# Where an attention and MLP kernel's buffers begin: first transfers on one queue, ten products of zeros, weights in one buffer each, and starts at multiples of 512 bytes

## The chip, the cores and the metric

The kernel runs on one core of one Trainium2 chip. The metric is the device time of one launch in microseconds (us), the median of several runs. A measurement of this kernel can tell about 0.3% from no change.

## What is computed

Everything is float32. With x of 2048 rows and 448 columns, 16 heads of 28 columns:

```python
g = sigmoid((x * gate_w).sum(-1, keepdims=True))
qkv = (x @ wqkv)                      # 448 -> 3 * 448, split into q, k, v of 16 heads
p = softmax(q @ k.T * 28 ** -0.5)     # per head, 2048 x 2048
a = concat_heads(p @ v) @ wo
y = layernorm(x)
b = gelu(y @ w1 + b1) @ w2 + b2       # 448 -> 1792 -> 448
out = g * a + (1 - g) * b
```

## The kernel before, in words

**Split numbers.** Most products run in the `F32R` type. An operand is kept as two parts, a rounded high part (`...h`) and the rest (`...l`), and a product is the sum of three: high by high, high by low, low by high. The 448 rows of a weight are laid out as 4 tiles of 128 rows; the last tile holds 64 rows twice, so that its low part lies in its own upper half and a sum of products takes 11 matrix products (three for each of tiles 0 to 2, two for tile 3), not 12. ScalarE makes the high parts, VectorE or GpSimd the low parts.

**Stages, in the order in which TensorE runs them** (TensorE's order, and in most stages that of all engines, is the order of the program text):

1. `WARM` = 8 products of zeros (L275 to L276), 128 by 128 float32, while the first transfers run.
2. q and k of the first 512 rows (L301 to L335). Seven tiles `m` of 128 weight columns (`wh[m]`, `wl[m]`) are multiplied by the four tiles `t` of x transposed (`xh[0]`, `xl[0]`). The order follows the arrival of the pieces: w0, x0, w1, x1, w2, x2, w3, x3, w4, w5, w6. `fetch_wqk` (L176) and `fetch_x` (L193) issue the transfers, all on SyncE's queue (SP) except x0, which goes on ScalarE's queue (L289). `split_wqk` (L180) and `split_x` (L197) make the parts.
3. The rest of q and k (`qk_tile`, L215, products at L222, 512 columns) and v (`v_tile`, L225, products at L234, 450 columns: 448 of v and one of the gate). q, k, v go to DRAM. VectorE takes the statistics of the layer norm meanwhile.
4. The MLP in four chunks of 512 rows: `mlp1` (L604, products at L612, 512 columns) and `mlp2` (L619, products at L625, L626, L630, 448 columns). Between them a "filler" (`RowMax`, L381) already computes the row maxima of the attention scores: products of 28 rows at L440, which VectorE reduces (L420, L422).
5. Attention in 16 blocks (4 groups of heads, 4 chunks of queries): scores in three products (L563, 28 or 29 rows; four heads lie in four groups of 32 rows and run beside each other), exponentials on ScalarE (L567), the rest of the filler, and probabilities by v (L828, plain float32).
6. The output projection (`project`, L725, products at L733 to L735, 448 columns) and the gate.

**Where the buffers lie.** Each `tile(...)` is a buffer with the same range of bytes in all 128 partitions. A pool stacks its buffers in the order in which the program makes them, each rounded up to 32 bytes, from the left end of the memory or (`side="right"`) from the right end. Before, this gives, in bytes of a partition:

- left: four small constants from 16384, `const` from 16512 to 18336, then `qx`, `qo`, `qw` and, later in the same place, the pools of the MLP and of attention. 18336 is 416 past a multiple of 512. So `raw`, `xh`, `xl`, `hl` (and later `hh`, `hl`, `h`, `pt`, `w2h`) start 416 past one, `wvh` too, `wvl` 448 past one, and the rows `t` of `wvh` and `wvl` follow each other at 1800 bytes. `wh0`, `wl0`, `wh1`, ... come after three small buffers (`st`, `mv`, `mr`) and start 96 past a multiple of 512. `w2l` and the results of attention (`oh0` to `ol2`) start 160 past one, since they follow buffers with rows of 1792 bytes.
- right: `khr` at 215392 (352 past a multiple of 512), and so `qd`, the `w1f` buffers, the two `y`, and in attention `khi`, `klo`, `qh`, `ql`, `vg`, all 352 past one.

Every start before is thus a multiple of 32 but, apart from `wvl`, of no larger power of two.

**What the MLP's buffers lie on.** The pools of the MLP reuse the bytes of `qx`, `qo`, `qw`; a buffer's first write waits until the last use of what lay there. `hh0`, the first one that `mlp1` writes (L615), lies over the last bytes of `qw`.

The lines that set the order of the first transfers and the zeros:

```python
zeros = spare(NF - 1)[:, 0, :P]
nc.vector.memset(zeros, 0.0)
for _ in range(WARM):
    nc.tensor.matmul(bank[:, 0, :P], zeros, zeros, start=True, stop=True)
...
for what, i in turns:
    if what == "w":
        fetch_wqk(i)
    else:
        fetch_x(0, i, nc.sync if i else nc.scalar)
```

Of the kernel before, what the change touches and what calls it, by code (L numbers as in the profile page):

```python
# [7 lines left out]
F32 = mybir.dt.float32  # L8
F32R = mybir.dt.float32r
AF = mybir.ActivationFunctionType  # L10
# [5 lines left out]
P = 128  # L16
# [6 lines left out]
CH = 512  # L23
# [4 lines left out]
NM = 2 * D // P  # L28
# [3 lines left out]
MLP_G = MLP_MAX // 260  # L32
MG = 6
FS = 4
WARM = 8
W1, W2 = 0.233, 0.205
LQ = 12
STEPS = (2, 5, 7, 8, 9, 10)
# [4 lines left out]
def kernel(ctx: ExitStack, tc: tile.TileContext, xt, wqk, wv, wo, xk, w1, b1, w2, b2,  # L43
                          ident_d, sel_d, out):
    nc = tc.nc

    const = ctx.enter_context(tc.tile_pool(name="const", bufs=1))
# [6 lines left out]
    gate = const.tile([P, NT], F32, name="gate")  # L54
    ngate = const.tile([P, NT], F32, name="ngate")
    zall = const.tile([P, NT], F32, name="zall")
    nc.vector.memset(eps_t, EPS)


# [9 lines left out]
    nc.vector.memset(one_t, 1.0)  # L69


    mpool = ctx.enter_context(tc.tile_pool(name="mpool", bufs=2, side="right"))

    khr = mpool.tile([P, S], F32R, name="khr", bufs=1)
# [83 lines left out]
    with tc.tile_pool(name="qx", bufs=2) as qx, tc.tile_pool(name="qo", bufs=4) as qo, \  # L158
# [3 lines left out]
        def next_ps():  # L162
            nonlocal nps
            nps += 1
            return bank[:, nps % 8]

        def raw():
            return qx.tile([P, CH], F32, name="raw", bufs=6)
# [2 lines left out]

            return mw1.tile([P, 2, CH], F32, name=f"w1f{i}")

        wh, wl, wt = {}, {}, {}

        def fetch_wqk(m):  # L176
            wt[m] = halves.pop(0).rearrange("p (t x) -> p t x", t=4)
            nc.sync.dma_start(wt[m], wqk[m])

        def split_wqk(m):  # L180
            wh[m] = qw.tile([P, 4, P], F32R, name=f"wh{m}")
            wl[m] = qw.tile([P, 4, P], F32R, name=f"wl{m}")
            nc.scalar.activation(wh[m], wt[m], AF.Copy)
            nc.gpsimd.tensor_sub(wl[m], wt[m], wh[m].bitcast(F32))

        wvh = qw.tile([P, 4, 450], F32R, name="wvh")
        wvl = qw.tile([P, 4, 450], F32R, name="wvl")
        vt = [qw.tile([P, H, 32], F32, name=f"vt{i}") for i in range(3)]

        xh, xl = {}, {}  # L190
        xraw = {}

        def fetch_x(c, t, queue=nc.sync):  # L193
            xraw[c, t] = raw()
            queue.dma_start(xraw[c, t], xt[t, :, c * CH:(c + 1) * CH])

        def split_x(c, t):  # L197
            if t == 0:
                xh[c] = qx.tile([P, 4, CH], F32R, name="xh")
                xl[c] = qx.tile([P, 3, CH], F32R, name="xl")  # L200
            r = xraw.pop((c, t))
            nc.scalar.activation(xh[c][:, t], r, AF.Copy)
            if t < 3:
                nc.vector.tensor_sub(xl[c][:, t], r, xh[c][:, t].bitcast(F32))
            else:
                nc.vector.tensor_sub(xh[c][64:128, t], r[64:128], xh[c][64:128, t].bitcast(F32))

        def qk_out(c, m, ps):
            hl = qo.tile([P, 2, CH], F32R, name="hl")
            nc.scalar.activation(hl[:, 0], ps, AF.Copy)  # L210
            nc.vector.tensor_sub(hl[:, 1], ps, hl[:, 0].bitcast(F32))
            nc.sync.dma_start(qk[:, m * P:(m + 1) * P, c * CH:(c + 1) * CH].rearrange("n p t -> p n t"),
                              hl.bitcast(F32))

        def qk_tile(c, m):  # L215
            ps = next_ps()
            ops = []
            for t in range(3):
                ops += [(wh[m][:, t], xh[c][:, t]), (wh[m][:, t], xl[c][:, t]), (wl[m][:, t], xh[c][:, t])]
            ops += [(wh[m][:, 3], xh[c][:, 3]), (wl[m][:, 3], xh[c][:, 3])]  # L220
            for i, (a, b) in enumerate(ops):
                nc.tensor.matmul(ps, a, b, start=(i == 0), stop=(i == len(ops) - 1))  # L222
            qk_out(c, m, ps)
# [50 lines left out]
# [3 lines that stand above are left out]
# [8 lines left out]
        for what, i in turns:  # L285
            if what == "w":
                fetch_wqk(i)
            else:
                fetch_x(0, i, nc.sync if i else nc.scalar)  # L289
        wvr = []  # L290
        for t in range(4):
            wvr.append(halves.pop(0)[:, :450])
# [1 line left out]
        for t in range(2):  # L294
            fetch_x(1, t)
# [3 lines left out]
        banks = [next_ps() for m in range(NM)]  # L299
        there, pieces, late, count = [], [], [], [0] * NM  # L300
        for what, i in turns:  # L301
            if what == "w":
                if i < 4:
                    split_wqk(i)
                there.append(i)
                new = [(i, t) for t in pieces]
            else:
                split_x(0, i)
                pieces.append(i)
                new = [(m, i) for m in there]  # L310
            ops = [("hh", m, t) for m, t in new]

            low, late = late + [("lh", m, t) for m, t in new], []
            if what == "w":
                late = [x for x in low if x[1] == i]
            ops += [x for x in low if x not in late]
            ops += [("hl", m, t) for m, t in new if t < 3]
            if i == NM - 1:
                ops += late
            for k, m, t in ops:  # L320
                a, b = wl[m] if k == "lh" else wh[m], xl[0] if k == "hl" else xh[0]
                nc.tensor.matmul(banks[m], a[:, t], b[:, t], start=(count[m] == 0), stop=(count[m] == 10))  # L322
                count[m] += 1
                if m == 0 and count[m] == 11:

                    for n in range(4, NM):
                        split_wqk(n)
                    for n in range(4):
                        nc.scalar.activation(wvh[:, n], wvr[n], AF.Copy)
                        nc.gpsimd.tensor_sub(wvl[:, n], wvr[n], wvh[:, n].bitcast(F32))  # L330
                if count[m] == 11:
                    qk_out(0, m, banks[m])
                    if m in (1, 3):
                        split_x(1, m // 2)
                        fetch_x(1, m // 2 + 2)  # L335
# [34 lines left out]
        for n in range(NM, 11 * NC):  # L370
            for what, a in ahead[n]:
                what(*a)
            c, m = divmod(n, 11)
            if m < NM:
                qk_tile(c, m)
            else:
                v_tile(c * TPC + m - NM)
            for what, a in behind[n]:
                what(*a)
# [218 lines left out]
    hh, hl = {}, {}  # L598
# [234 lines left out]
    with tc.manual_schedule(engines=ENGINES):  # L833
# [7 lines left out]
        while u < 4 * steps:  # L841
# [4 lines left out]
            while at < units[-1] // 4:  # L846
                at += 1
                n, k = divmod(at, NT)
                g, c = divmod(n, NC)
# [111 lines left out]
```

## Time and profile before

| | |
|---|---|
| median of 3 runs | 1117.81 us (1117.55 to 1120.91) |
| the profiled execution | 1117.1 us, its span 1115.3 us |
| granted TensorE clock | 1.0 |
| VectorE (DVE), busy share of the span | 66% |
| ScalarE (ACT), busy share | 57% |
| GpSimd (POOL), busy share | 30% |
| DMA, mean rate over the span | 76 GB/s |

The span is the time from the first to the last instruction; the 1.8 us beside it lie outside the program. A row of the chain of waits reads: start, time, engine, output buffer, line, count; `PE bank L222 x76` are 76 products of line 222 that followed each other with nothing between. Time divided by count is the **pace**: the distance from one product to the next. The profile's own duration of one product is longer than its pace, because a product starts while the one before still drains. A row of the timeline reads: start, time, engine, line, operation, output and inputs, count, and in brackets the idle time before it with what ended it. `SPq` and `ACTq` are transfers that an engine's queue issues. A float32 product at `F32` appears as two rows.

### The profile page before, as it was taken

How to read it: one execution, taken by the hardware profiler on the slowest of the kernel's cores; microseconds unless marked ns; L12 is line 12 of the kernel's file. 1: busy time of each engine (PE TensorE's matmuls, PEld its weight loads, DVE VectorE, ACT ScalarE, POOL GpSimd, SP SyncE). 2: the span in 40 equal slices, each digit the busy share in tenths (PEclk: the TensorE clock that was granted, in tenths of full speed). 3: DMA queues.
4: the chain of work that ended last, by engine and by line, in shares of the span. 5: the costliest groups of instructions: out<-in, count | busy, mean ns of one | idle time of the engine just before them, and what ended most of it. 6: DMA issues, size and time to landing. Idle time of an engine off the chain costs nothing.

```text
span 1115.3 us, 19794 instructions
## 1 busy us (share of the span) xinstructions
PE 1106.8 (99%) x8152; PEld 674.9 (61%) x8152; DVE 741.2 (66%) x1030; ACT 634.8 (57%) x660; POOL 334.0 (30%) x354
## 2 busy tenths in 40 slices
PE   9999999999999999999999999999999999999998
PEld 7888777777777777744444444444444444454546
DVE  4553398988888889576766766666667767746103
ACT  5334651330231232287887887887878878847572
POOL 5016664242344231013112221320223024342350
PEclk9999999999999999999999999999999999999999
DMA  7988641011121023162100220012021003002011
GB/s 247 363 266 284 179 122 53 9 47 36 50 55 37 25 53 87 41 166 79 28 19 20 61 72 19 21 28 52 26 59 37 18 20 94 12 26 69 34 53 58
DMA packets 53079, 84.35 MB, mean 76 GB/s; under 512 B 8516, under 2 KB 28500, under 8 KB 52076
## 3 DMA queue, kind: packets, MB, share of 16 engines
q1 hardware_dynamic: 48588, 76.01, 22.2%
q0 software_dynamic: 4256, 6.81, 2.3%
q8 instruction: 64, 1.05, 0.4%
q10 hardware_dynamic: 144, 0.26, 0.1%
q14 instruction: 27, 0.22, 0.1%
HBM read 56.40 MB, written 26.49 MB: 74 GB/s over the span
## 4 chain that ended last, share of the span: by engine, by line
PE 98%; DVE 1%; ACT 1%; DMA 0%; issue 0%; ACTq 0%
PE bank L828 22%; PE bank L563 20%; PE bank L440 16%; PE bank L612 13%; PE bank L222 5%; PE bank L630 5%; PE bank L625 4%; PE bank L626 4%; PE bank L234 3%; PE bank L322 2%; PE bank L733 1%; PE bank L734 1%; PE bank L735 1%; DMA w1f<-in_wqk 0%; ACT khi L567 0%
## 5 line engine op out<-in xcount | busy, mean ns | idle before, releaser
L567 ACT ACTIVATE pt<-bank 128x1536 f32<-128x1536 f32 (+1 forms) x386 | 460.3, 1243 | 121.7 <-PE bank L563 121.7
L420 DVE TENSOR_REDUCE mx<-bank 128x1 f32<-128x512 f32 x618 | 409.8, 688 | 174.0 <-PE bank L440 160.1
L828 PE MATMUL bank<-pt,vg 128*32 128x512 f32 x1942 | 260.4, 602 | 0.0
L422 DVE TENSOR_REDUCE mx<-bank 128x2 f32<-128x1024 f32 x203 | 238.9, 1220 | 30.3 <-PE bank L440 30.0
L440 PE MATMUL bank<-khi,qd 28*128 28x512 f32 x512 | 241.9, 480 | 0.1
L440 PEld LDWEIGHTS bank<-khi,qd 28*128 28x128 f32 x512 | 92.3, 181 | 148.1 <-DVE mx L420 104.4
L563 PE MATMUL bank<-qh,klo 28*128 28x512 f32 x1024 | 174.2, 394 | 0.0
L563 PE MATMUL bank<-qh,khi 29*128 29x512 f32 x768 | 156.3, 480 | 0.8 <-ACT khi L567 0.6
L612 PE MATMUL bank<-y,w1f 128*128 128x512 f32 x616 | 151.9, 397 | 0.0
L612 PEld LDWEIGHTS bank<-y,w1f 128*128 128x128 f32 x616 | 112.6, 188 | 33.1 <-issue 10.8
L563 PE MATMUL bank<-ql,khi 28*128 28x512 f32 x768 | 128.8, 390 | 0.0
L617 POOL TENSOR_TENSOR hl<-h,hh 128x512 fp32r<-128x512 f32 x56 | 72.5, 1295 | 117.6 <-ACT h L616 77.4
L615 ACT ACTIVATE hh<-bank,b1s 128x512 fp32r<-128x512 f32 x56 | 38.7, 691 | 98.6 <-PE bank L612 98.6
L828 PEld LDWEIGHTS bank<-pt,vg 128*32 128x32 f32 x1942 | 44.6, 108 | 78.7 <-issue 78.3
L563 PEld LDWEIGHTS bank<-qh,klo 28*128 28x128 f32 x1024 | 87.2, 185 | 3.6
L636 ACT ACTIVATE h<-bank 128x448 f32<-128x448 f32 x16 | 8.7, 546 | 137.9 <-PE bank L630 103.6
L749 POOL DMA_DIRECT2D lt<-ob x15 | 10.9, 727 | 253.0 <-DVE ob L748 253.0
L630 PE MATMUL bank<-w2h,hl 128*128 128x448 f32 x224 | 85.0, 379 | 0.0
L563 PEld LDWEIGHTS bank<-qh,khi 29*128 29x128 f32 x768 | 60.6, 181 | 39.8 <-ACT pt L567 25.0
L625 PE MATMUL bank<-w2h,hh 128*128 128x448 f32 x224 | 83.3, 372 | 0.0
L626 PE MATMUL bank<-w2l,hh 128*128 128x448 f32 x224 | 81.9, 366 | 0.0
L440 PE MATMUL bank<-khr,qd 28*128 28x512 f32 x512 | 80.3, 467 | 0.5 <-issue 0.3
(135 smaller groups left out, 1298.0 us busy)
## 6 DMA issues: line engine op xcount, KB each, us to landing
qk<-hl SPq DMA_DIRECT2D x28, 512.0 KB
vs<-vt SPq DMA_DIRECT2D x16, 256.0 KB
s<-in_xt SPq DMA_DIRECT2D x16, 256.0 KB
raw<-in_xt SPq DMA_DIRECT2D x15, 256.0 KB
rc<-rls POOLq DMA_DIRECT2D x60, 64.0 KB, 2.2
w1f<-in_xk SPq DMA_DIRECT2D x8, 448.0 KB
gbs<-h SPq DMA_DIRECT2D x16, 224.0 KB
klo<-qk SPq DMA_DIRECT2D x16, 224.0 KB
```

The costliest lines, as they stand in the source:

```text
L222: nc.tensor.matmul(ps, a, b, start=(i == 0), stop=(i == len(ops) - 1))
L420: nc.vector.reduce_max(self.mx[:, c0:c0 + 1], bank[:, b0], axis=AX)
L422: nc.vector.reduce_max(self.mx[:, c0:c1 + 1:c1 - c0], bank[:, b0:b1 + 1], axis=AX)
L440: nc.tensor.matmul(bank[:, b], self.qds[self.n][r, i * P:(i + 1) * P], khi[self.n // NC][r, k * 512:(k + 1) * 512], start=True, stop=True)
L563: nc.tensor.matmul(bank[:, p], a[r, k * P:(k + 1) * P], b[r], start=(i == 0), stop=(i == 2))
L567: nc.scalar.activation(t, bank[:, at[0]:at[-1] + 1], AF.Exp, scale=SCALE)
L612: nc.tensor.matmul(ps, a, b, start=(i == 0), stop=(i == len(ops) - 1))
L617: nc.gpsimd.tensor_sub(hl[f], h, hh[f].bitcast(F32))
L625: nc.tensor.matmul(a, hh[f][:, sl], w2h[f], start=(f == 0), stop=False)
L626: nc.tensor.matmul(a, hh[f][:, sl], w2l[f], start=False, stop=False)
L630: nc.tensor.matmul(a, hl[f][:, sl], w2h[f], start=False, stop=(f == NF - 1))
L828: nc.tensor.matmul(pv[32 * j:32 * j + 32, :], vg[n // NC][:, k, 32 * j:32 * j + 32], probs.pop(4 * step + j), start=(k == 0), stop=(k == N ...
```

## The change

- `WARM` goes from 8 to 10.
- `fetch_x` loses its `queue` argument: x0 is issued on SP's queue too, between w0 and w1.
- `wh` and `wl` become one buffer each, `[P, NM, 4, P]`, made before `wvh`; product and split take the slice `[:, m]` or `[:, m, t]`.
- `wvh` and `wvl` are made with rows of 512 elements (2048 bytes), of which 450 are used.
- An unused buffer of 96 bytes ends `const`, and an unused pool of 352 bytes begins the right side. `qx` then starts at 18432 and `khr` at 215040, both multiples of 2048. All the buffers listed above with 416, 352, 96 or 448 start at a multiple of 512; `w2l` and `oh0` to `ol2`, behind rows of 1792 bytes, start 256 past one. The small buffers `st`, `mv`, `mr` and the rows of the layer norm now end `qw`, with `vt0` to `vt2` before them, so `hh0` lies over `vt2`.

The number, the order and the operands of all other instructions stay as they are.

```diff
-WARM = 8
+WARM = 10
...
     zall = const.tile([P, NT], F32, name="zall")
+    const.tile([P, 24], F32, name="pad")
...
+    ctx.enter_context(tc.tile_pool(name="edge", bufs=1, side="right")).tile([P, 88], F32, name="edge")
     mpool = ctx.enter_context(tc.tile_pool(name="mpool", bufs=2, side="right"))
...
-        wh, wl, wt = {}, {}, {}
+        wh = qw.tile([P, NM, 4, P], F32R, name="wh")
+        wl = qw.tile([P, NM, 4, P], F32R, name="wl")
+        wt = {}
...
         def split_wqk(m):
-            wh[m] = qw.tile([P, 4, P], F32R, name=f"wh{m}")
-            wl[m] = qw.tile([P, 4, P], F32R, name=f"wl{m}")
-            nc.scalar.activation(wh[m], wt[m], AF.Copy)
-            nc.gpsimd.tensor_sub(wl[m], wt[m], wh[m].bitcast(F32))
-
-        wvh = qw.tile([P, 4, 450], F32R, name="wvh")
-        wvl = qw.tile([P, 4, 450], F32R, name="wvl")
+            nc.scalar.activation(wh[:, m], wt[m], AF.Copy)
+            nc.gpsimd.tensor_sub(wl[:, m], wt[m], wh[:, m].bitcast(F32))
+
+        wvh, wvl = (qw.tile([P, 4, CH], F32R, name=f"wv{x}")[:, :, :450] for x in "hl")
...
-        def fetch_x(c, t, queue=nc.sync):
+        def fetch_x(c, t):
             xraw[c, t] = raw()
-            queue.dma_start(xraw[c, t], xt[t, :, c * CH:(c + 1) * CH])
+            nc.sync.dma_start(xraw[c, t], xt[t, :, c * CH:(c + 1) * CH])
...
-                ops += [(wh[m][:, t], xh[c][:, t]), (wh[m][:, t], xl[c][:, t]), (wl[m][:, t], xh[c][:, t])]
-            ops += [(wh[m][:, 3], xh[c][:, 3]), (wl[m][:, 3], xh[c][:, 3])]
+                ops += [(wh[:, m, t], xh[c][:, t]), (wh[:, m, t], xl[c][:, t]), (wl[:, m, t], xh[c][:, t])]
+            ops += [(wh[:, m, 3], xh[c][:, 3]), (wl[:, m, 3], xh[c][:, 3])]
...
-                fetch_x(0, i, nc.sync if i else nc.scalar)
+                fetch_x(0, i)
...
-                a, b = wl[m] if k == "lh" else wh[m], xl[0] if k == "hl" else xh[0]
-                nc.tensor.matmul(banks[m], a[:, t], b[:, t], start=(count[m] == 0), stop=(count[m] == 10))
+                w, x = wl if k == "lh" else wh, xl[0] if k == "hl" else xh[0]
+                nc.tensor.matmul(banks[m], w[:, m, t], x[:, t], start=(count[m] == 0), stop=(count[m] == 10))
```

## Prediction

> **What bounds the kernel now.** First the page: the busy times, then the chain that ended last.
>
> ```profile
> PE 1106.8 (99%) x8152; PEld 674.9 (61%) x8152; DVE 741.2 (66%) x1030; ACT 634.8 (57%) x660; POOL 334.0 (30%) x354
> ...
> PE 98%; DVE 1%; ACT 1%; DMA 0%; issue 0%; ACTq 0%
> PE bank L828 22%; PE bank L563 20%; PE bank L440 16%; PE bank L612 13%; PE bank L222 5%; PE bank L630 5%; PE bank L625 4%; PE bank L626 4%; PE bank L234 3%; PE bank L322 2%; PE bank L733 1%; PE bank L734 1%; PE bank L735 1%; DMA w1f<-in_wqk 0%; ACT khi L567 0%
> ```
>
> TensorE is the chain, from its first real product to the end. So time can come from two places only: the few us before it runs without a gap, and the pace of its products. The pace is read from the chain of waits in windows in which one stage runs alone (start, us, what, count):
>
> ```profile
> 10.90 14.20 PE bank L322 x62
> ```
> ```profile
> 26.24 7.80 PE bank L234 x38
> ```
> ```profile
> 35.28 17.74 PE bank L222 x76
> ```
> ```profile
> 65.98 13.05 PE bank L222 x57
> ```
> ```profile
> 116.35 14.76 PE bank L612 x65
> ```
>
> Time by count: L322 229.0 ns, L234 (450 columns) 205.3, L222 233.4 and 229.0, L612 227.1 ns. The projection (448 columns) from the first and the last of 37 steps of the timeline:
>
> ```profile
> 1103.46 0.37 PE L734 MATMUL bank<-wol,oh 128*128 128x448 f32 x1
> ...
> 1110.97 0.37 PE L735 MATMUL bank<-woh,ol 128*128 128x448 f32 x1
> ```
>
> 7.51 / 37 = 203.0 ns. Is that the array's own speed? The start of the program tells:
>
> ```profile
> 8.76 0.63 PE L322 MATMUL bank<-xl,wh 128*128 128x512 f32 x1
> ...
> 9.19 1.01 PE L322 MATMUL bank<-xh,wh 128*128 128x512 f32 x2
> ...
> 10.04 0.86 PE L322 MATMUL bank<-xh,wl 128*128 128x512 f32 x3
> ```
>
> Up to 10.04 us a product of 512 columns takes 0.43 us, behind it about 0.229 with the same buffers: the clock steps up. Half of 0.427 is 213.5 ns. If the step doubles the clock, which I take from these two paces, the array needs 213.5 ns, and 13.6 (L612) to 19.9 ns (L222) of each pace is an excess that the slow clock hides. Something that doesn't speed up with the array, such as the reading of operands, may set it. 213.5 ns for the 2048 bytes of a row is 6.67 ns for 64 bytes; in this unit the excess is 2.0 for L612, 2.3 to 3.0 for L222, 2.4 for L733 to L735 (186.8 ns by columns) and 2.7 for L234 (187.6).
>
> **The change, part by part.**
>
> *Starts at multiples of 512 (or 256).* A row of 2048 bytes that begins 32 past a multiple of 64, as all of them do before, covers 33 pieces of 64 bytes instead of 32, one of 1792 bytes 29 instead of 28. If reading goes by such pieces, a product loses one unit, 6.67 ns. v's rows of 1800 bytes cover 29 pieces from each old and new start: nothing there. No row of before has a 512-column product on an aligned operand, so the price is unknown; the bounds are nothing and the whole excess, 13.6 ns and more, and below nothing as in the last rival. I take one unit, as it is what the layout itself gives. How many products:
>
> ```profile
> L222 PE MATMUL bank<-xh,wh 128*128 128x512 f32 x84 | 33.4, 397 | 0.0
> L222 PE MATMUL bank<-xh,wl 128*128 128x512 f32 x84 | 33.2, 395 | 0.0
> L222 PE MATMUL bank<-xl,wh 128*128 128x512 f32 x63 | 24.9, 395 | 0.0
> ```
> ```profile
> L612 PE MATMUL bank<-y,w1f 128*128 128x512 f32 x616 | 151.9, 397 | 0.0
> L630 PE MATMUL bank<-w2h,hl 128*128 128x448 f32 x224 | 85.0, 379 | 0.0
> ...
> L440 PE MATMUL bank<-khr,qd 28*128 28x512 f32 x476 | 63.2, 466 | 0.5 <-issue 0.3 <-DVE mx L422 0.2
> ```
>
> L222 has 231, L322 77 (7 x 11 in the text), L612 616, L625, L626 and L630 three times 224, L733 to L735 three times 64: 1788 products of 128 rows, one behind the other. 1788 x 6.67 ns = 11.9 us.
>
> The products of 28 rows are less sure. One group of attention:
>
> ```profile
> 587.71 0.72 PE L563 MATMUL bank<-qh,khi 29*128 29x512 f32 x4
> 588.05 0.62 PE L563 MATMUL bank<-qh,klo 28*128 28x512 f32 x4
> ...
> 588.99 0.49 PE L440 MATMUL bank<-khi,qd 28*128 28x512 f32 x1
> 589.40 1.06 PE L828 MATMUL bank<-pt,vg 128*32 128x512 f32 x8
> 590.40 0.50 PE L440 MATMUL bank<-khi,qd 28*128 28x512 f32 x1
> ```
>
> Several heads run at once, and the 2.69 us of the group hold steps of 0.34 and 0.41 us at the changes of shape, which no start explains. With one unit in each of 7 levels of the about 205 groups (3072 products of L563 by 15) it would be 9.6 us, in the MLP's 476 filler products 3.2 us. Between 0 and 12.8 us I take 0, because beside the 128-row products nothing shows here what a level waits for; 12.8 stays in the range.
>
> What hides a gain: VectorE in the MLP, ScalarE in attention.
>
> ```profile
> 201.00:379.00 178.00, 178.00 (x911) 133.35 (x909) 157.71 (x165) 43.69 (x71) 66.63 (x52) 1.00 0.14 39
> 480.00:985.00 505.00, 504.93 (x4782) 237.77 (x4775) 346.95 (x550) 403.95 (x342) 124.29 (x171) 1.00 0.17 44
> ```
>
> The busy times are those of TensorE, its loads, VectorE, ScalarE, GpSimd. VectorE has 157.71 of 178 us in the MLP, so TensorE can gain 11% there before the filler's reductions are late; ScalarE 403.95 of 505 in attention. One unit is 3%.
>
> *First transfers and zeros.*
>
> ```profile
> 0.72 0.40 ACTq L195 DMA_DIRECT2D raw<-in_xt  x1
> ...
> 0.72 0.86 SPq L178 DMA_DIRECT2D w1f<-in_wqk  x2
> ...
> 1.20 3.78 PE L276 MATMUL bank<-w1f 128*128 128x128 f32 x16 [1.20 <-DVE w1f L274]
> ...
> 5.15 0.63 ACT L183 ACTIVATE wh<-w1f 128x512 fp32r<-128x512 f32 x1 [2.71 <-DMA w1f<-in_wqk]
> ...
> 5.69 0.61 ACT L202 ACTIVATE xh<-raw 128x512 fp32r<-128x512 f32 x1
> ...
> 6.36 0.79 PE L322 MATMUL bank<-xh,wh 128*128 128x512 f32 x1 [1.37 <-ACT xh L202]
> 6.83 0.63 ACT L202 ACTIVATE xh<-raw 128x512 fp32r<-128x512 f32 x1
> ```
>
> x0 is now issued 0.43 us later, and the SP transfers behind it by as much; w0 no longer shares its first us. ScalarE waits for w0 until 5.15 us, x0 is there when its turn comes. The first product can come up to 0.35 us earlier, or 0.1 us later if x0 is late. Two more zeros are four rows of at most 3.78 / 16 = 0.24 us: they end by 5.9 us, ahead of 6.36, so they delay nothing; the idle 1.4 us shrink. If the clock's step then comes earlier, the 6.6 products between 7.2 and 10.04 us save 0.2 us each, 1.3 us at most. Sum between -1.6 and +0.1; I take -0.5 us.
>
> *One buffer for wh, for wl.* No instruction is added. A wait could be: a split of `wh[:, 1]` behind the products of `wh[:, 0]`. But `xh` is such a buffer already, and at 6.83 ScalarE writes its second slice without idle time, half a us after the first product began to read the first. Nothing.
>
> *hh0 over vt2.*
>
> ```profile
> 114.12 0.55 ACT L236 ACTIVATE vt<-bank 128x448 f32<-128x448 f32 x1 [1.19 <-PE bank L234]
> 116.44 0.55 ACT L236 ACTIVATE vt<-bank 128x448 f32<-128x448 f32 x1 [1.77 <-PE bank L234]
> ...
> 118.91 0.69 ACT L615 ACTIVATE hh<-bank,b1s 128x512 fp32r<-128x512 f32 x1 [0.63 <-PE bank L612]
> ```
>
> vt2 holds v tile 14, written until 114.67; its transfer has 4.2 us until `hh0` is written. Were it late, ScalarE's later work queues behind L615, but only the third tile of L612, 2.5 us later, needs that bank again. Nothing.
>
> The sum against the profiled execution's 1117.1 us (span 1115.3 and 1.8 beside it, 0.7 below the median): 1117.1 - 11.9 - 0.5 = 1104.7; with the 0.7, **1105.4 us**.
>
> **The rivals.**
>
> *Starts don't matter (0.28).* v's own rows speak for it: they start 0, 8, 16 and 24 bytes past a multiple of 32 for its four tiles.
>
> ```profile
> 28.34 0.37 PE L234 MATMUL bank<-wvh,xh 128*128 128x450 f32 x1
> ...
> 28.95 0.37 PE L234 MATMUL bank<-wvh,xh 128*128 128x450 f32 x1
> ...
> 29.57 0.36 PE L234 MATMUL bank<-wvh,xh 128*128 128x450 f32 x1
> ...
> 30.18 0.37 PE L234 MATMUL bank<-wvh,xh 128*128 128x450 f32 x1
> ```
>
> Three products take 0.61, 0.62, 0.61 us: no tile is faster. And L222 has 233.4 and 229.0 ns with the same weights' buffers, so part of the excess moves with unmoved starts. Against it: all old starts are alike modulo 64, and 1800 bytes can't show the piece. Then only the start is left: 1117.8 - 0.5 = 1117.3 us. The Trainium skill, "SBUF — State Buffer", Specifications (TRN2), gives lines of 16 bytes, of which each new one costs something. By that rule starts at multiples of 32 lose nothing, and the change gives this rival's time; the equal tiles of v agree.
>
> *The whole excess goes (0.12).* Then about two units leave every product: 1788 + 176 + 476 + 205 x 7 = 3875 x 13.3 ns = 51.5 us, 1065.8 us with the start. For it: 2.0 units of L612 are all alike. Against: v's 2.7 units, and the two paces of L222. The Trainium skill, "TensorE: Matmul & The Clock Gate", Back-to-back issue gap, gives 512 / 2.4 + 2.5 = 216 ns for a 512-column product (an estimate from its formula); the trace's 227.1 to 233.4 differ, and by the page the rest is removable.
>
> *Both operands begin at the same place and get in each other's way (0.20).* With all starts at 0 of 512, the weights' load and the moving operand of each product read the same place at once. Price: the slow pace of L222, 3.0 units, everywhere: L612 616 x 6.3 ns = 3.9, the 448-column ones 864 x 3.8 = 3.3, L222 about 0.4, and one unit in fillers and levels 12.8: 20.4 us, 1138 us; without the last, 1125. It decides if L612 goes from 227 to above 230. Against it: `y` and `w1f` both start at 352 of 512 already, and theirs is the fastest pace; `xh` (416) and `wh` (96) differ, and theirs is the slowest.
>
> **How the numbers follow.** The forecast, one unit in the 128-row products and up to that in the others (1090 to 1114), has 0.40. A measurement can tell about 0.3%, 3.4 us, from no change. Faster is 0.40 + 0.12, same 0.28, slower 0.20. The range of 8 in 10 runs from 1062, which cuts off the low end of the second rival, to 1127, which holds the mild form of the last and leaves out its full form.
>
> **What would show it.** Right: L612 at about 220 ns and L222 at 223 to 227, L733 to L735 at 196, L234 unchanged at 205; the first product by 6.4 us. L612 still at 227 and L222 at 229 to 233 are the first rival, 214 to 216 the second, L612 over 230 the third. In attention a group's 2.69 us tells whether the levels gain. Wrong I would be above all if the excess belongs to the change of weights between products, whose loads (x8152) stand beside every product.

## The result, and the profile after

The changed kernel takes 1115.51 us (median of 17 runs, 1115.0 to 1120.98); the kernel before takes 1117.81 us beside it (17 runs, 1116.15 to 1120.91). The ratio is 0.998, with a 95% interval of 0.9970 to 0.9989. So it is faster by 2.3 us, not by the 12.4 us of the forecast. The interval doesn't reach 1, but 2.3 us are less than the 0.3% (3.4 us) that the prediction took as the least that a measurement can tell. The profiled execution took 1115.45 us, its span is 1113.7 us; that is 1.6 us less than the profiled execution of before, while the medians lie 2.3 us apart. The lines named here have moved by one: L222 is now L223, L612 is L613.

The page of the changed kernel, busy times and chain:

```profile
PE 1105.7 (99%) x8156; PEld 675.7 (61%) x8156; DVE 745.5 (67%) x1030; ACT 634.8 (57%) x660; POOL 333.3 (30%) x354
...
PE 96%; DVE 2%; DMA 1%; ACT 1%; issue 0%; POOL 0%; SPq 0%; ACTq 0%; DVEq 0%
```

TensorE is still the chain; 4% of it belong to others, where it was 2%. Its paces, from the chain of waits in windows of one stage (start, us, what, count):

```profile
25.01 8.95 PE bank L235 x44
```
```profile
33.96 17.50 PE bank L223 x77
```
```profile
63.15 14.98 PE bank L223 x66
```

L235 (v) goes at 203.4 ns instead of 205.3, L223 (q, k) at 227.3 and 227.0 instead of 233.4 and 229.0. The MLP and the projection, from the timeline:

```profile
114.55 4.27 PE L613 MATMUL bank<-y,w1f 128*128 128x512 f32 x18
```
```profile
1101.87 0.37 PE L735 MATMUL bank<-wol,oh 128*128 128x448 f32 x1
...
1109.38 0.37 PE L736 MATMUL bank<-woh,ol 128*128 128x448 f32 x1
```

L613: less the 0.40 us of the last one's own row, 3.87 us for 17 steps, 227.6 ns, as before (227.1). The projection: 37 steps in 7.51 us, 203.0 ns, to the digit as before. So the MLP and the projection, whose starts moved from 32 past a multiple of 64 to a multiple of 64 as those of q and k did, gained nothing.

The start, from the timeline of the changed kernel:

```profile
1.20 4.63 PE L277 MATMUL bank<-w1f 128*128 128x128 f32 x20 [1.20 <-DVE w1f L275]
6.28 0.80 PE L323 MATMUL bank<-xh,wh 128*128 128x512 f32 x1 [0.44 <-ACT xh L203]
6.87 0.53 PE L323 MATMUL bank<-xh,wl 128*128 128x512 f32 x1
7.24 0.40 PE L323 MATMUL bank<-xl,wh 128*128 128x512 f32 x1
```

The zeros fill more of the gap (0.44 us idle instead of 1.37), the first product comes at 6.28 us (6.36 before), and the clock has stepped up by 7.24 us instead of 10.04.

Where the time went, by the starts of the stages in the two traces (us; own sums over the starts of TensorE's products):

| | before | after | difference |
|---|---|---|---|
| first v product | 26.08 | 24.85 | -1.23 |
| first product of the MLP | 116.19 | 113.63 | -2.56 |
| length of the first `mlp1` stage | 39.92 | 40.86 | +0.94 |
| whole MLP, to the first product of probabilities by v | 355.44 | 356.54 | +1.10 |
| from there to the end | 643.66 | 643.50 | -0.16 |
| end | 1115.29 | 1113.67 | -1.62 |

At the MLP's start 2.56 us are won: 1.2 up to the first v product, above all by the earlier clock, and 1.3 by the paces of q, k and v. Of these the MLP's first stage gives nearly one back. The prediction took 0.5 us for the start and had no term for a stage that gives time back. Two questions follow: what sets the paces, if not the start, and what takes the gain back.

### The profile page after: what moved, and what is told of

Read it like the earlier page. It is cut to its first block, busy times and chain, and to the rows that moved or that the text cites. A ratio compares the mean times of both kernels' runs of the same rounds, so it can differ in the third digit from the quotient of the medians.

```text
span 1113.7 us, 19805 instructions
## 1 busy us (share of the span) xinstructions
PE 1105.7 (99%) x8156; PEld 675.7 (61%) x8156; DVE 745.5 (67%) x1030; ACT 634.8 (57%) x660; POOL 333.3 (30%) x354
## 4 chain that ended last, share of the span: by engine, by line
PE 96%; DVE 2%; DMA 1%; ACT 1%; issue 0%; POOL 0%; SPq 0%; ACTq 0%; DVEq 0%
PE bank L829 22%; PE bank L564 20%; PE bank L441 15%; PE bank L613 12%; PE bank L223 5%; PE bank L631 5%; PE bank L626 4%; PE bank L627 4%; PE bank L235 3%; PE bank L323 1%; PE bank L734 1%; PE bank L735 1%; PE bank L736 1%; DVE mx L423 1%; DMA raw<-in_xt 1%
## 5 line engine op out<-in xcount | busy, mean ns | idle before, releaser
L441 PE MATMUL bank<-khi,qd 28*128 28x512 f32 x512 | 241.7, 479 | 0.1
L441 PEld LDWEIGHTS bank<-khi,qd 28*128 28x128 f32 x512 | 92.5, 182 | 148.1 <-DVE mx L421 105.2
L613 PE MATMUL bank<-y,w1f 128*128 128x512 f32 x616 | 152.3, 398 | 0.2 <-ACT h L617 0.2
L613 PEld LDWEIGHTS bank<-y,w1f 128*128 128x128 f32 x616 | 112.6, 188 | 33.4 <-issue 10.6
L441 PE MATMUL bank<-khr,qd 28*128 28x512 f32 x512 | 80.8, 468 | 0.4 <-DVE mx L423 0.2
```

The source lines that it names most:

```text
L441: nc.tensor.matmul(bank[:, b], self.qds[self.n][r, i * P:(i + 1) * P], khi[self.n // NC][r, k * 512:(k + 1) * 512], start=True, stop=True)
```

## Experiments

All ratios are against runs of the kernel before on the same chip, with their 95% intervals.

**The parts by themselves.** The zeros alone, on the kernel before (`a1_zeros`):

```diff
-WARM = 8
+WARM = 10
```

> The kernel before with ten products of zeros instead of eight, nothing else. Theory (the zeros bring the clock's step forward): the step from a pace of 0.43 to 0.23 us comes near 7.2 us instead of 10.0, the stage from the first real product to the first v product falls from 19.7 us to 18.2 to 18.6, the time from 1117.8 to about 1116.5 us. Rival (it is the queue that makes the start shorter): the step stays at 10.0, the stage at 19.7, the time at 1117.8.

1117.15 us, ratio 0.9998 (0.9988 to 1.0008). The first v product comes at 25.06 us, 1.0 earlier than before, but in this execution the first MLP stage takes 41.59 us instead of 39.92: more than all of it is given back. The one queue alone (`a2_queue`):

```diff
-                fetch_x(0, i, nc.sync if i else nc.scalar)
+                fetch_x(0, i)
```

> The kernel before with x0 on SP's queue, nothing else. Theory: w0 is there earlier, but x1, w2 and the pieces behind them land 0.7 to 0.9 us later, the stage up to the first v product is as long as before or up to 0.5 us longer, the time 1117.8 to 1118.4 us. Rival (the queue makes the start shorter): stage 18.6 us, time 1116.6.

1118.30 us, ratio 1.0006 (0.9995 to 1.0016). The first product is 0.43 us earlier, the first v product 0.14 later, since the other pieces come later. The layout alone (`a3_layout`), with the other two parts undone:

```diff
-WARM = 10
+WARM = 8
...
-                fetch_x(0, i)
+                fetch_x(0, i, nc.sync if i else nc.scalar)
```

> The changed kernel with eight zeros and x0 on ScalarE's queue: the layout alone. Theory (the layout takes the pace of the q, k, v products from 229 to 233 down to 227 ns, and hh0 over vt2 gives part back): q, k, v after the first stage 1.4 us shorter, the first MLP stage 40.8 instead of 39.9 us, the time 1117.2 us. Rival 1 (the pace has nothing to do with the layout): paces of 229 to 233 ns, 1117.8 or more. Rival 2 (nothing is lost at hh0, the MLP's weights were only late for a stage that began earlier): first MLP stage 40.0 to 40.3, time 1116.5.

1116.59 us, ratio 0.9992 (0.9984 to 1.0000): about 0.9 us. q, k and v have the paces of the changed kernel (227.5 and 203.3 ns), the MLP begins 1.21 us earlier, and its first stage loses 0.64. The three ratios multiply to 0.9996, not to 0.998. Each has an interval of about 0.001 to either side, so this difference isn't clear of noise, and whether the parts add isn't shown.

**What takes the gain back.** The first suspect was `hh0` over vt. In the changed kernel ScalarE's table load (`ACT_TABLE_LOAD`, which stands ahead of the first gelu) comes late (timelines of ScalarE, the kernel before and the changed one):

```profile
117.00 1.28 ACT L615 ACT_TABLE_LOAD   x1
118.91 0.69 ACT L615 ACTIVATE hh<-bank,b1s 128x512 fp32r<-128x512 f32 x1 [0.63 <-PE bank L612]
```
```profile
116.40 1.28 ACT L616 ACT_TABLE_LOAD   x1 [1.97 <-PE bank L613]
117.69 0.69 ACT L616 ACTIVATE hh<-bank,b1s 128x512 fp32r<-128x512 f32 x1
```

Before, the load runs in the gap ahead of the first tile's end and `hh0` starts on time. After, ScalarE sits idle for 1.97 us and loads the table when the tile is already done; the third tile of L613 then has to wait until L617 has freed its bank (waits of TensorE in the changed kernel's first MLP stage: us in total, times, longest):

```profile
PE bank L613 <- ACT h L617: 0.2, 1, 0.2
PE bank L441 <- issue: 0.2, 1, 0.2
```

By the starts of TensorE's products this stop costs 0.46 us: two steps of 581 and 337 ns where 228 are usual. It is in all ten traces in which `hh0` lies over vt2 and in none of the nine others. The rest of the 0.94 us, 0.47, is lost at the first products of L441, where the changed kernel waits longer than the one before. So `a4_vt_first` makes vt ahead of the weights, and `hh0` lies over the end of `wvl`:

```diff
+        vt = [qw.tile([P, H, 32], F32, name=f"vt{i}") for i in range(3)]
         wh = qw.tile([P, NM, 4, P], F32R, name="wh")
...
-        vt = [qw.tile([P, H, 32], F32, name=f"vt{i}") for i in range(3)]
```

> The changed kernel with vt0 to vt2 made before wh and wl, so that hh0 lies over the end of wvl and not over vt2. Theory (ScalarE's wait for vt2's transfer puts its table load behind the first product of the MLP): the table load starts before the first MLP product ends, no stall at the third tile, the first MLP stage back at 39.9 to 40.1 us instead of 40.9, the time 1114.6 us. Rival (weights late for a stage that begins earlier): 40.6 to 40.9 us, the time 1115.5.

1114.83 us, ratio 0.9976 (0.9967 to 0.9985), which can't be told from the changed kernel's 0.998. The wait at the third tile is gone and the table load starts at 115.57 us, ahead of the first tile's end. But the profiled execution, which was the slowest of its 12 (1118.86 us), shows another (timeline of TensorE, then busy times by stretches, with the granted clock third from the end):

```profile
129.62 0.50 PE L441 MATMUL bank<-khr,qd 28*128 28x512 f32 x2
131.01 0.50 PE L441 MATMUL bank<-khr,qd 28*128 28x512 f32 x1 [0.88 <-DMA s<-in_w]
132.18 0.50 PE L441 MATMUL bank<-khr,qd 28*128 28x512 f32 x3 [0.67 <-issue]
```
```profile
129.90:133.30 3.40, 1.85 (x9) 1.00 (x8) 1.84 (x2) 0.15 (x1) 2.00 (x2) 1.00 0.66 209
133.30:136.70 3.40, 3.40 (x10) 2.62 (x9) 3.40 (x4) 2.09 (x4) 1.28 (x1) 0.50 0.22 80
```

The first products of the filler wait 1.55 us, and behind the stretch in which TensorE was busy for 1.85 of 3.40 us the clock is granted at half for the next stretch: 10 products there, 17 in the 3.40 us ahead of the wait. The first MLP stage takes 43.29 us. The next theory: the keys that L441 reads are fetched late (GpSimd issues them at tile 1), at a time that doesn't move with TensorE. Three kernels start the filler one tile later; on the changed kernel (`c1_filler_later`):

```diff
-FS = 4
+FS = 5
```

> The changed kernel with FS 5 in place of 4: the first products of the filler (L441) come one tile of the first MLP stage, 11 products or 2.5 us, later. Theory: the changed kernel reaches the MLP 2.56 us earlier, but the keys that the filler's first products read are fetched by GpSimd at tile 1 and land 5.8 to 10.3 us later, by a time that doesn't move with TensorE; so TensorE waits at L441 (0.3 us there in the changed kernel, 2.0 us with the zeros alone, 2.0 us with vt first, where one window of 3.4 us at half clock follows). Then the first MLP stage is 40.86 - 0.3 to - 0.5 = 40.4 to 40.6 us, the median 1114.6 to 1115.3 and the highest runs (1117.1 to 1121.0 in the changed kernel) come down below 1117. Rival: the loss is ScalarE's wait for hh0 over vt and nothing else; then the stage stays at 40.9, the median at 1115.5, and the high runs stay.

1119.74 us, ratio 1.0014 (1.0004 to 1.0024): slower, and the theory misses. The first MLP stage does fall, to 39.02 us, but the wait comes back behind it (timeline of TensorE, then of VectorE):

```profile
159.94 0.50 PE L441 MATMUL bank<-khr,qd 28*128 28x512 f32 x2 [0.65 <-DVE mx L423]
161.07 0.50 PE L441 MATMUL bank<-khr,qd 28*128 28x512 f32 x2 [0.63 <-DVE mx L423]
162.20 0.64 PE L441 MATMUL bank<-khr,qd 28*128 28x512 f32 x2 [0.63 <-DVE mx L423]
```
```profile
155.69 1.56 DVE L121 TENSOR_TENSOR w2l<-more,w2h 128x448 fp32r<-128x448 f32 x1
157.18 1.57 DVE L121 TENSOR_TENSOR w2l<-s,w2h 128x448 fp32r<-128x448 f32 x1
158.67 5.74 DVE L423 TENSOR_REDUCE mx<-bank 128x2 f32<-128x1024 f32 x5
```

VectorE still splits weights when the filler's products need their banks reduced, and again a stretch at half clock follows. With vt first as well (`c2_vt_filler`, `a4_vt_first` with FS 5):

> The changed kernel with vt ahead of wh (hh0 then doesn't wait for vt's copies) and FS 5. Theory: both waits of the first MLP stage are gone, so the stage is 39.7 to 40.0 us against 40.86 in the changed kernel and 43.29 in the profiled run of vt first alone; no gap of over 0.9 us between two products, no window at half clock behind the first one; median 1113.8 to 1114.6, highest below 1116.5. It would be the best of all so far (vt first alone: 1114.83). Rival: the keys are no bound, then 1114.8 as vt first alone, with its high runs.

1115.67 us, ratio 0.9976 (0.9967 to 0.9986), above the 1113.8 to 1114.6 us expected. The first stage takes 38.48 us and the MLP 355.27, no longer than the 355.44 before, with no window at half clock; in attention this execution lost 1.4 us by steps of about 0.25 us, one in each 94 us, which no other trace shows and whose cause stays open. And the kernel before with FS 5 (`c3_before_later`):

> The kernel before with FS 5. Theory: before reaches L440 at 131.0 us, 2 us later than the changed kernel, and waits only 0.3 to 0.5 us there in its profiled run; the median falls by 0.2 to 0.8 us (to about 1116.7 to 1117.2 beside 1117.4), and the runs above 1119 go. Rival, the keys are no bound: no difference.

1117.03 us, ratio 0.9998 (0.9990 to 1.0006): not to be told from no difference. Last, the keys' fetch one tile earlier, on `a4_vt_first` (`d1_keys_early`):

```diff
-                    if f == 1:
+                    if f == 0:
                         load_khr(0, queue=nc.gpsimd)
```

> The changed kernel with vt ahead of wh, FS 4, and the keys' fetch at tile 0 of the first MLP stage instead of tile 1, about 2.7 us earlier. Theory: the wait at the filler's first products (2.0 us at 131 us in the profiled run of vt first, with a window at half clock behind it) is for these keys; it goes, the first MLP stage takes 39.4 to 40.0 us (43.29 there), the median is 1113.8 to 1114.6 and the highest run below 1116.5. Rival: VectorE's reduce is what the filler waits for, because VectorE still splits second weights; then the waits stay at 1 to 2 us and the median at 1114.8 with runs of 1116 to 1119.

1115.51 us, ratio 0.9975 (0.9965 to 0.9986). The wait at L441 is gone, as the theory says; the first stage takes 41.04 us, against it. The waits between 113 and 140 us:

```profile
ACT w1f L108 <- DMA more<-in_w: 2.8, 1, 2.8
...
PE bank L613 <- ACT h L617: 1.4, 1, 1.4
```

Now the weights' transfer is late, ScalarE waits for it in its order, and the activation behind it holds a bank of TensorE. The busy times of before and of this kernel side by side say why (the last two columns: DMA share and GB/s):

```profile
113.00:121.00 8.00, 8.00 (x39) 6.88 (x38) 0.52 (x3) 3.64 (x5) 2.08 (x2) 1.00 0.48 142
121.00:130.00 9.00, 9.00 (x41) 7.48 (x40) 3.38 (x2) 7.42 (x13) 8.83 (x10) 1.00 0.95 264
```
```profile
113.00:121.00 8.00, 8.00 (x37) 6.65 (x36) 0.16 (x1) 4.37 (x6) 3.13 (x4) 1.00 0.95 239
121.00:130.00 9.00, 7.60 (x33) 5.74 (x31) 1.55 (x2) 6.65 (x12) 5.26 (x5) 1.00 0.53 176
```

The DMA engines are at 0.95 in the one stretch or in the other: here the keys, put first, made the weights late. The share alone is no limit, since in the kernel before TensorE is busy for all of the 9.00 us beside it. What the traces show is that a TensorE which reaches the MLP 1.0 to 2.7 us earlier meets waits in its first stage: for the table load, for keys, for weights, for VectorE, which still splits weights. They take the gain back, and which of them costs most differs from run to run. That transfers and splitting together set a limit for this stage is argued, not shown; `c2_vt_filler`, with no late table load and no wait at the filler's first products, gives nothing back in the MLP.

**What sets the pace.** Theory B is the prediction's (starts), theory A says that the place of a product's loaded operand against its moving one counts, modulo 128 bytes. (In q and k the weights are loaded and x moves; in v, the second MLP and the projection the weights move.) The kernel before has distance 64 between x (416) and the q, k weights (96), distances of 0 to 56 in v, and distance 0 in the MLP (352 and 352; 416 and 416) and the projection (416 and 160, that is 256): the stages whose distance the change alters are the ones whose pace changed. The modulus is a guess at first. `b1_both_416` takes the pad of 24 elements out of the changed kernel, so that x and all weights on the left lie at 416 together:

```diff
-    const.tile([P, 24], F32, name="pad")
```

> The changed kernel without its pad of 24 elements: all buffers on the left begin at 416 past a multiple of 512 bytes again, x's and the weights' alike (before: x at 416, q and k's weights at 96, v's at 416). The MLP's left buffers too; the right side stays aligned. Theory A, the distance between the two operands of a product counts (equal modulo 128): L223 goes at 226.7 ns as in the changed kernel, and L235 at 203.3. Theory B, starts at a multiple of 64 count (the step of my prediction, for these products alone): L223 229 to 233 ns and the q, k stages 17.9 to 18.1 us instead of 17.5 to 17.8. The second MLP products (L626, L627, L631), at 416 here and at 0 in the changed kernel, keep 203.4 ns under both, as they did between before and after.

The chain of waits in the q, k stage:

```profile
36.24 17.50 PE bank L222 x77
```

227.3 ns: both operands start 32 past a multiple of 64, as before, at the distance of after, and they have the pace of after. Theory B falls, as it does with the MLP and the projection above. (The one time, 1117.53 us, belongs to an execution with a window at half clock at 9.1 us, below; its first v product comes 2.3 us later than in the changed kernel.) Then x at 0, the weights at 64 (`b2_wh_64`), and at 96 (`b3_wh_96`, 24 elements):

```diff
+        qw.tile([P, 16], F32, name="gap")
         wh = qw.tile([P, NM, 4, P], F32R, name="wh")
```

> The changed kernel with 64 bytes put ahead of the q, k weights: x begins at 0 past a multiple of 512, the weights at 64; both at multiples of 64. Theory A, the distance between the two operands modulo 128 counts (before: 64, L222 at 229 to 233; both at 416, distance 0: 227.4): L224 goes at 229 to 233 ns, the q, k stages take 17.9 to 18.1 us. Theory B2, the weights' own place counts (32 past a multiple of 64 is bad only for them, or 96 past a multiple of 128): 227.4 ns, 17.5 to 17.8 us.

> The changed kernel with 96 bytes put ahead of the q, k weights: x at 0, the weights at 96 past a multiple of 512, their own place as before. Theory A (distance, here 96 modulo 128): not 227.4 but 228 to 233. Theory B2 (the weights' own place): 229 to 233 ns as before. Taken with the run at 64: A alone if both are slow, B2 alone if only this one is; if neither is slow, both fall and the cause is x's place at 416 together with the weights' at 96.

One time each: 1116.26 and 1118.57 us. The chain of waits, first at 64, then at 96:

```profile
34.22 17.96 PE bank L224 x77
```
```profile
35.31 18.03 PE bank L224 x77
```

233.2 and 234.2 ns. With both operands at a multiple of 64 the products are as slow as before. v moved too: 200.4 ns at 64, 207.7 at 96, 203.3 at 0, so the best distance isn't the same for 450 columns as for 512.

One rival is left by these runs, the weights' own place modulo 128: fast at 0 and 32, slow at 64 and 96. The kernel before answers it: `y` and `w1f` both start at 352, which is 96 past a multiple of 128, and L612 goes at 227.1 ns. For 448 and 450 columns no run separates the distance from the weights' own place.

Nor is the distance all that counts. In the kernel before, L222 goes at 233.3 ns behind v's products and at 229.1 ns behind a pair of small transposes (L266, at 64.7 and again at 101.9 us) in the middle of a stage, with the same buffers; these are the two paces of the prediction's rows. `b2_wh_64`, at the same distance modulo 128, stays at 233.3 behind them. (Modulo 256 the distances differ, 192 before and 64 here.)

`b4_halves` asks what the rest of the excess belongs to. At c = 1 each product is done as two of 256 columns, at c = 2 only 64 columns of the weights are used:

```diff
+                    if c == 1:
+                        x, o = b[:, n * 256:(n + 1) * 256], ps[:, n * 256:(n + 1) * 256]
+                    if c == 2:
+                        w, o = a[:, :64], ps[:64]
```

> The changed kernel with two other q, k stages. In the first stage behind the start (c = 1) each product is done in two halves of 256 columns of x, in the next (c = 2) only 64 of the 128 columns of the weights are used, so half of that chunk's q and k isn't computed; c = 3 stays. [...]

The chain of waits at c = 1 and at c = 2:

```profile
35.94 15.12 PE bank L229 x126
```
```profile
64.56 15.19 PE bank L229 x66
```

120.0 ns for 256 columns. By half of the cold pace (213.5 ns for 512) the array needs 106.7, so 13.3 ns are left over, where 512 columns leave 13.8. Half of 227.3 would have been 113.7. That speaks for a price paid per product and not per column read, but it doesn't settle it: something besides the columns bounds short products. The last zeros of `e1_scan`, 128 columns of type `F32` with the clock already full, follow each other at 111 to 112 ns, where a quarter of 213.5 is 53, and 120.0 isn't far above that. 64 columns of weights take 230.2 ns against 227.0 in the same window of the changed kernel, so a shorter load doesn't make it smaller.

**Does each distance have its pace?** Two scans put the weights of each tile at another distance, in one kernel (`e1_scan` at 0, 32, 64, 96; `e2_scan` at 16, 48, 80, 112; v's rows at steps of 16 through both, and the second MLP's weights by `f`):

```diff
+        for m, d in enumerate([16, 16, 16, 16, 16, 16, 16]):
+            if d:
+                qw.tile([P, d // 4], F32, name=f"gap{m}")
+            wh.append(qw.tile([P, 4, P], F32R, name=f"wh{m}"))
+            wl.append(qw.tile([P, 4, P], F32R, name=f"wl{m}"))
```

> The changed kernel with the weights set apart in steps: q, k weights of tile m at 32, 64, 96, 0, 32, 64, 96 modulo 128 (x at 0), v's rows at 0, 16, 32, 48, the second MLP's weights by f at 0, 32, 64, 96 and so on (its hh and hl at 0). So one run gives a pace for each distance. Theory A with a curve (so far for 512 columns: 0 is 227.5, 64 is 233.4, 96 is 234.1; for 450: 0 is 203.3, 64 is 200.4, 96 is 207.7): the same values come back for L230 at 0, 64 and 96, and for L634 to L639 (448 columns) the pace varies with f, 200 at one distance and 207 at another. Rival: the pace hangs on the whole layout (which rows of the buffers, not the distance): no order by distance within one run, L634 to L639 at 203 for every f.

> As the scan before, at the distances between: q, k weights at 16, 48, 80, 112 by tile, v's rows at 64, 80, 96, 112, the second MLP's weights at 16 and 48 or 80 and 112. Theory A: values between those of the neighbours at multiples of 32 (227.5 to 234.1 for L231, 64 gives 200.4 and 96 gives 207.7 again for v's rows). Rival: one value for all.

One time each: 1116.62 and 1117.57 us. The chain of waits in the q, k stage of the first:

```profile
34.79 17.89 PE bank L230 x77
```

232.3 ns for the mixture. Its seven tiles lie at 32 to 224 in steps of 32 and go at 232.0, 233.8, 233.1, 231.6, 233.2, 228.6 and 233.2 ns. Modulo 128 this contradicts theory A: the tiles at 64 and 192 should be alike, and the one at 128 should have the 227 of a stage at 0. Modulo 256 it doesn't: 64 and 96 go about as in `b2_wh_64` and `b3_wh_96`, 192 about as the kernel before behind the transposes (229.1), and no tile lies at 0. The second scan has 230.4 to 233.3. So for q and k the scans don't decide between theory A with a larger modulus and the rival. The second MLP's products did differ in the first scan: 200.5 to 201.2 ns at 64 modulo 128 (L634, L635), 202 to 204 at the others. Two versions put whole stages at one distance: `f1_wv64_w2_64`, on `a4_vt_first`, with q, k at 0, v's weights and the second MLP's at 64, and `f2_wv112_w2_64` with v's at 112. Beside them ran the changed kernel once more (`f0_after_again`).

```diff
+        qw.tile([P, 16], F32, name="gap")
         wvh, wvl = (qw.tile([P, 4, CH], F32R, name=f"wv{x}")[:, :, :450] for x in "hl")
...
+    mw2.tile([P, 16], F32, name="gap2")
     for f in range(NF):
...
+    mw2.tile([P, 112], F32, name="gap3")
```

> The changed kernel itself, unchanged, for a comparison on the same chip with the two versions that run with it: 1115.1 to 1115.9 by its earlier runs (1115.51), under every theory.

> The changed kernel with vt ahead of wh, the second MLP's weights 64 bytes behind hh and hl modulo 128, and v's weights 64 behind x. Theory, the place of one operand against the other sets the pace, with its own best distance for each length: L235 goes at 200.4 ns instead of 203.3 (176 products, 0.5 us), L626 to L631's successors at 200.5 to 201.2 instead of 203.4 (672 products, 1.5 to 1.9 us), q and k stay at 227.5; so 2.0 to 2.4 us less than vt first alone, 1112.4 to 1113.3, under both kernels. Rival, the pace belongs to the stream as a whole, and one distance in a scan of mixed ones says nothing of a stream at that distance: the second MLP's products stay at 203 and the median at 1114.3 to 1115.3.

> As the run before with v's weights at 112 instead of 64. Theory: 197.2 ns for L235 (seen for 16 pairs in the scan), 0.5 us less than with 64. Rival: the scan's value doesn't hold for a stream of one distance; 203 to 208 ns, 0.5 to 1.3 us more than with 64.

f0: 1115.33 us, ratio 0.9982 (0.9974 to 0.9991). f1: **1112.16 us**, ratio 0.9956 (0.9943 to 0.9970). f2: 1112.67 us, ratio 0.9959 (0.9945 to 0.9973). The second MLP, timelines of the changed kernel and of f1:

```profile
191.82 0.36 PE L626 MATMUL bank<-w2h,hh 128*128 128x448 f32 x1
...
194.46 0.37 PE L627 MATMUL bank<-w2l,hh 128*128 128x448 f32 x1
```
```profile
189.73 0.36 PE L629 MATMUL bank<-w2h,hh 128*128 128x448 f32 x1
...
192.34 0.37 PE L630 MATMUL bank<-w2l,hh 128*128 128x448 f32 x1
```

13 steps each: 2.64 us and 2.61 us, 203.1 and 200.8 ns; over all such steps 203.4 (f0 too) and 200.2. At 672 products that is 2.2 us, and f1's MLP takes 353.83 us against 356.17 in f0. v in f1, from its chain of waits:

```profile
24.95 8.83 PE bank L236 x44
```

200.7 ns. In f2 v has 204.7, not the 197.2 that the second scan showed for 16 steps at 112: that value from a mixed stage didn't hold for a whole one. f1 is faster than both kernels. Of its lead over f0 of 3.2 us, 2.2 belong to the second MLP's pace and 0.45 to v's (176 x 2.55 ns); f1 also lacks the stop of 0.46 us that `hh0` over vt2 brings.

## Why the prediction was wrong

The step that failed is "If reading goes by such pieces, a product loses one unit, 6.67 ns": the term of 1788 x 6.67 = 11.9 us. Reading by pieces is not what the excess is. `b1_both_416` starts 32 past a multiple of 64, as before, and has the new pace; `b2_wh_64` starts at multiples of 64 and has the old one. So the term is not one of 1788 products at 6.67 ns: 231 of L223 gained 4.2 ns each (231.7 to 227.5 over all of them), 77 of L323 2.3, 176 of L235 1.9, together 1.5 us. The other 1480, the MLP and the projection, gained nothing, for their operands were at distance 0 before and after. That L612 was already at 227.1 on starts of 352 stood in the prediction's own rows, and in its last rival it was even put in words: `y` and `w1f` at the same place have the fastest pace, `xh` and `wh`, which differ, the slowest. I read this as an argument against a collision and not as the rule itself. That q, k and v gained at all is luck in the terms of the forecast: the new layout happened to bring their operands to distance 0. The direction came out right by this luck and by the earlier clock.

- **"Nothing there" for v** was wrong in a small way: 205.3 to 203.4 ns.
- **Zeros and queue, "I take -0.5 us", 1.3 at most**: the clock's step came as early as the bound allowed, and the first v product 1.23 us earlier. In the four traces with eight zeros the step lies at 10.0 to 10.7 us, with ten at 4.1 to 7.2 in 14 of 15 (in `a4_vt_first` at 10.45).
- **hh0 over vt2, "Nothing"**: it costs 0.46 us in each trace that has it. The prediction priced the wait on L615 itself and missed that the table load then no longer runs ahead of the first tile's end.
- **"What hides a gain"** looked at VectorE and ScalarE over the whole MLP. The gain is hidden in its first stage: 0.46 us by the late table load and 0.47 by waits at the filler's first products.
- **The excess belongs to the change of weights between products**: this was named as what would make the forecast wrong above all, and `b4_halves` speaks for it: products of 256 and of 512 columns exceed the array's time by 13.3 and 13.8 ns. That it is the change of weights isn't shown.
- **The rivals**: "starts don't matter" gave 1117.3 us, and by starts it was right; but the change moved a distance as well. "The whole excess goes" was wrong: no stage here came below 226.6 ns for 512 columns, where the formula of the Trainium skill, "TensorE: Matmul & The Clock Gate", Back-to-back issue gap, would give 216 (an estimate from it). The collision was wrong in sign for 512 columns, where equal places are the fastest; with 448 and 450 columns a distance of 64 is 3 ns faster than 0, but the change made no such distance.

## What to carry to other kernels

Where back-to-back products go slower than half of their cold pace, compare the stages by the distance between the starts of the loaded and the moving operand, not by the starts alone; try a few distances, a whole stage at each, since a mixed scan can mislead. A gain upstream is worth what the next stage can take: before costing it, look at how the next stage begins: here, with transfers at a share of up to 0.95 and with a backlog on VectorE. Where a buffer moves, look also at what the engine does just ahead of the first write to it, here a table load that lost its cover.

## What the runs showed of the hardware

**The clock goes by windows, up and down.** The clock's changes in a trace lie multiples of 3.41 us apart, at another phase in each execution. `b1_both_416`, by its own windows (busy TensorE second, clock third from the end):

```profile
2.24:5.65 3.41, 3.41 (x17) 3.30 (x16) 0.00 (x0) 0.98 (x2) 1.27 (x1) 1.00 0.75 222
5.65:9.06 3.41, 2.12 (x6) 0.78 (x5) 0.69 (x1) 1.54 (x3) 1.27 (x1) 1.00 0.99 345
9.06:12.48 3.42, 3.37 (x8) 2.69 (x9) 2.71 (x3) 3.32 (x6) 2.68 (x2) 0.50 1.05 403
```

(The 1.00 of the first row is no reading: the trace records the clock from its first change, at 5.65 us.) After a window full of zeros the clock steps up at 5.65 us; TensorE then waits for pieces of x, is busy for 2.12 of 3.41 us, and has half the clock in the next window. So zeros that raise the clock before the data can keep TensorE busy can lose it again. In `a1_zeros` a window with 2.38 us busy kept the clock:

```profile
128.64:132.05 3.41, 2.38 (x10) 1.24 (x8) 1.28 (x2) 0.96 (x2) 3.41 (x3) 1.00 1.01 197
132.05:135.46 3.41, 2.99 (x14) 2.36 (x15) 2.48 (x3) 2.02 (x4) 0.91 (x2) 1.00 0.63 191
```

Lost were those with 2.12, with 1.85 (in `a4_vt_first`) and, in `c1_filler_later`, with 1.50 us:

```profile
159.00:162.41 3.41, 1.50 (x8) 0.55 (x6) 3.41 (x4) 0.00 (x0) 0.15 (x1) 1.00 0.71 207
162.41:165.82 3.41, 3.41 (x10) 2.76 (x9) 3.13 (x3) 0.00 (x0) 2.39 (x2) 0.50 0.00 0
```

Yet in `e2_scan` a window with 1.80 us busy (6.71 to 10.12 us) kept it, so the busy time of the profile doesn't decide alone, and the exact condition stays open. A window at half clock costs up to 1.7 us, half of 3.41 (an estimate). The waits at the filler's first products straddled two windows in `a1_zeros`, and the clock stayed; in `a4_vt_first` they fell into one. The highest runs of the changed kernel (1117.1, 1118.3 and 1121.0 us) list a mean clock of 0.997 to 0.998 where the others have 0.999 to 1.0, which such windows would give; they have no trace. The Trainium skill, "TensorE: Matmul & The Clock Gate", HAM oscillation, warns of idle gaps over about 3.4 us; here three gaps of about 0.65 us each, in one window, were enough (`c1_filler_later`), and the measurement decides.

**A stream can hold a pace.** In the kernel before, the pace of q and k is 229.1 ns instead of 233.3 for the rest of a stage once two transposes have come in between, in all four traces with that layout. The 227 ns are seen only in whole stages at distance 0. What state the stream keeps, modulo how many bytes the distance counts, and why 512 columns are faster at 0 than at 64 and 450 or 448 the other way round, no run here shows.
